# Attention ahead of two expert layers: the first pass one slot further ahead, the rows of maxima behind the products with v

## The chip, the cores and the metric

The kernel runs on one core of a Trainium2 chip. TensorE (PE in the profile, its weight loads PEld) multiplies, VectorE (DVE), ScalarE (ACT) and GpSimd (POOL) do the rest, and SyncE (SP) issues the DMAs. Each engine works through its own list of instructions in order; between engines there are semaphores. The metric is the device time of the whole program in microseconds, the median of several runs.

## The reference, cut to what matters

Queries are averaged in pairs, then attended over 1152 keys per head; what follows (two expert layers, called MoE below) is the same before and after the change.

```python
B, H, S, D = q.shape                              # 4, 8, 1152, 64
q_pool = q.reshape(B, H, S // 2, 2, D).mean(axis=3)      # 576 queries per head
scores = 1.0 / np.sqrt(D) * np.matmul(q_pool, k.transpose(0, 1, 3, 2))
scores = scores - np.max(scores, axis=-1, keepdims=True)
attn = np.exp(scores)
attn = attn / (np.sum(attn, axis=-1, keepdims=True) + 1e-09)
attn_out = np.matmul(attn, v)                     # then moe, then soft moe
```

## The kernel before

**Pairs, phases, slots.** The heads of a batch are taken two at a time: 16 pairs, each with two phases (one head each), each with nine slots (128 keys each). The loop over `s` runs through all slots; `u` is the slot's place in its pair, 0 to 17, `c` its place in its phase. The order of PE, ACT, DVE and POOL is the order of the program text (a manual schedule); the DMA queue on SP is ordered by the framework.

**Two passes.** The softmax needs each query's maximum before the exponentials. The first pass (`emit_S`, L189 and L190) multiplies 128 queries with 384 keys and lets DVE reduce the product to maxima, 27 such steps per pair; its products rotate through two buffers (`ps_s`). They are taken from one long list: `first()` emits the next. There is one `first()` in every slot and a second in every even slot, so the first pass runs ahead of the second by as many steps as were emitted before the loop. When all maxima of a group are there, `emit_nm` (L193, DVE) makes their negatives, and `emit_row` (L202 PE, L206 or L208 ACT) turns them with a matmul into a row that is copied into the tile `q2`. The second pass (`emit_E`, L218) multiplies keys with `q1` and with `q2` (which subtracts the maximum), and ACT takes the exponential (L221). `x0 = 1, n = 4` is the group of one head; `x0 = 0, n = 1` is a remainder of both heads of the next pair.

**Behind it.** POOL adds up the exponentials (`acc`, L225 and L227). In even slots PE multiplies the exponentials of two earlier slots with v (`emit_PV`, L234, eight matmuls); `emit_sum` (L244), `emit_recip` (L250, DVE) and `emit_O` (L259, L260, DVE) make the quotient of the phase before.

**The next pairs' operands.** `pool_q` (L105, two POOL additions) sums neighbouring queries into the tile `qp` at the end of slot u = 17, for the pair after next. `kq8` (L133, L109) transposes the last key block and the last query block at u = 1; its result is read by ACT (L140, L158, L159) and DVE (L141, L161). `q_bank` (L109, L118, L120) transposes the other query blocks, `k0` and `k4` (L133, L140, L141) the other key blocks, `kd_dma` (L168, L169) and `q2_dma` (L175) spread them by DMA. Transposes, rows and sums all take their output from `bank()`, which in the loop is the single buffer of the pool `ps_t`: the next user waits until the last reader of the one before is done.

```python
ps_s = ctx.enter_context(tc.tile_pool(name="ps_s", bufs=2, space=PSUM))
ps_t = ctx.enter_context(tc.tile_pool(name="ps_t", bufs=1, space=PSUM))
...
st["qp"] = kq_p.tile([128, 9, 2, 64], F32, tag="qp", name="qp")
```

Of the kernel before, what the change touches and what calls it, by code (L numbers as in the profile page):

```python
# [23 lines left out]
def attention(ctx, nc, tc, q, k, v, xa, ident, ones, hooks):  # L24
# [18 lines left out]
    NPH = 2 * NPAIR  # L43
# [36 lines left out]
    def load_v(pi):  # L80
        b, hp = pairs[pi]
        t = v_p.tile([128, 2, 9, 64], F32, tag="vr", name="vr")
        nc.sync.dma_start(
            out=t.rearrange("p h c d -> p h (c d)"),
            in_=v[b, 2 * hp:2 * hp + 2].rearrange("h (p c) d -> p h (c d)", c=9),
        )
        raws["v"][pi] = t
# [4 lines left out]
    def bank():  # L92
        if front[0]:
            return ps_e.tile([128, 512], F32, tag="se", name="t")
        return ps_t.tile([128, 512], F32, tag="t", name="t")
# [3 lines left out]
    def pool_q(pi, u):  # L99
        st = prep.setdefault(pi, {})  # L100
        if u == 0:
            st["qp"] = kq_p.tile([128, 9, 2, 64], F32, tag="qp", name="qp")
        qr = raws["q"][pi]
        eng = nc.gpsimd if pi else nc.vector
        eng.tensor_tensor(out=st["qp"][:, :, u, :], in0=qr[:, :, 0, :], in1=qr[:, :, 1, :], op=ALU.add)  # L105
# [7 lines left out]
    def q_bank(pi, g):  # L113
        st, ps = prep[pi], bank()
        q_tr(pi, 4 * g, 4, ps, 0)
        src = ps.rearrange("p (j h x) -> p h j x", j=4, h=2)
        o = st["q1"][:, :, g, :256].rearrange("p h (j x) -> p h j x", x=64)
        nc.scalar.copy(o, src)  # L118
        for h in range(2):
            nc.vector.tensor_tensor(  # L120
                out=o[64:128, h], in0=src[64:128, h], in1=o[64:128, h].bitcast(F32), op=ALU.subtract
            )
# [22 lines left out]
    def k0(pi):  # L145
        k_bank(pi, 0, 4, bank())

    def k4(pi):
        k_bank(pi, 4, 4, bank())

    def kq8(pi):
        ps = bank()
        k_bank(pi, 8, 1, ps)
        o, st = qd[pi % 2], prep[pi]
        src = ps[:, 128:256].rearrange("p (h g x) -> p h g x", h=2, g=2)
        q1 = st["q1"][:, :, :, 256:]
        for h in range(2):
            nc.scalar.copy(o[64 * h:64 * h + 64, 64 * h:64 * h + 64], ps[64 * h:64 * h + 64, 128 + 64 * h:192 + 64 * h])  # L158
        nc.scalar.copy(q1, src)  # L159
        for h in range(2):  # L160
            nc.vector.tensor_tensor(  # L161
                out=q1[64:128, h], in0=src[64:128, h], in1=q1[64:128, h].bitcast(F32), op=ALU.subtract
            )

    def kd_dma(pi, h):
        st, t = prep[pi], KD[(2 * pi + h) % 3]
        src = st["kp"][64 * h:64 * h + 64].bitcast(F32)
        nc.sync.dma_start(out=t[64:128, 0].bitcast(F32), in_=src[:, 0])  # L168
        ins = nc.sync.dma_start(out=t[0:64].bitcast(F32), in_=src)  # L169
        last_dma[0] = ins.ins  # L170
        return ins.ins

    def q2_dma(pi):
        st = prep[pi]
        return nc.sync.dma_start(out=st["q2"][0:64].bitcast(F32), in_=st["q1"][0:64].bitcast(F32)).ins  # L175


    def emit_S(ph, x, n):
        pi, h = divmod(ph, 2)
        st = prep[pi]  # L180
        if ph not in M_:
            M_[ph] = sm_p.tile([128, 5, 3], F32, tag="m3", name="m3")
        if x == 0:
            w, r = qd[pi % 2], st["kp"][:, 0]
        else:
            g, u = divmod(x - 1, 2)
            w, r = st["q1"][:, h, g, 128 * u:128 * u + 128], KD[ph % 3][:, 0]
        ps = ps_s.tile([128, 512], F32, tag="S", name="S")[:, :384]
        nc.tensor.matmul(ps, lhsT=w, rhs=r[:, 384 * n:384 * n + 384], start=True, stop=True)  # L189
        nc.vector.tensor_reduce(out=M_[ph][:, x, n:n + 1], in_=ps, axis=AX.X, op=ALU.max)  # L190

    def emit_nm(ph, x0, n):
        nc.vector.tensor_reduce(  # L193
            out=NM[ph % 2][:, x0:x0 + n, 64], in_=M_[ph][:, x0:x0 + n], axis=AX.X, op=ALU.max, negate=True
        )

    def emit_row(ph, x0, n):
        pi, h = divmod(ph, 2)
        q2 = prep[pi]["q2"][64:128]
        ps = bank()  # L200
        for x in range(n):
            nc.tensor.matmul(  # L202
                ps[:, 128 * x:128 * x + 128], lhsT=NM[ph % 2][:, x0 + x], rhs=identr, start=True, stop=True
            )
        if x0 == 0:
            nc.scalar.copy(q2[:, :, :, 256:], ps[64:128, :128].rearrange("p (h g x) -> p h g x", h=2, g=2))  # L206
        else:
            nc.scalar.copy(q2[:, h, :, :256], ps[64:128].rearrange("p (g x) -> p g x", g=2))  # L208


    def emit_E(ph, c):
        pi, h = divmod(ph, 2)
        st, kd = prep[pi], KD[ph % 3]
        e = E_[ph, c] = e_p.tile([128, 2, 288], F32, tag="e", name="e")
        for g in range(2):
            ps = ps_e.tile([128, 512], F32, tag="se", name="se")[:, :288]
            for z, y in enumerate((st["q1"], st["q2"])):
                nc.tensor.matmul(  # L218
                    ps, lhsT=kd[:, z, 128 * c:128 * c + 128], rhs=y[:, h, g], start=z == 0, stop=z == 1
                )  # L220
            nc.scalar.activation(out=e[:, g], in_=ps, func=AF.Exp, scale=1.0 / 16)  # L221

        if c == 1:
            acc_[ph] = sm_p.tile([128, 2, 288], F32, tag="acc", name="acc")
            nc.gpsimd.tensor_tensor(out=acc_[ph], in0=E_[ph, 0], in1=e, op=ALU.add)  # L225
        elif c > 1:
            nc.gpsimd.tensor_tensor(out=acc_[ph], in0=acc_[ph], in1=e, op=ALU.add)  # L227

    def emit_PV(ph, c):
        pi, h = divmod(ph, 2)  # L230
        if c == 0:
            O_[ph] = ps_o.tile([128, 512], F32, tag="o", name="o")
        for g in range(2):
            nc.tensor.matmul(  # L234
                O_[ph][64 * g:64 * g + 64, :288], lhsT=raws["v"][pi][:, h, c, :], rhs=E_[ph, c][:, g],
                start=c == 0, stop=c == 8,
            )
        E_.pop((ph, c))
# [9 lines left out]
    def emit_recip(ph, u):  # L248
        r = R_[ph][:, 144 * u:144 * u + 144]
        nc.vector.reciprocal(out=r, in_=r)  # L250
# [31 lines left out]
    def first(n=1):  # L282
        for _ in range(n):
            if firsts:
                emit_S(*firsts.pop(0))
# [4 lines left out]
    emit_row(0, 0, 1)  # L290
    emit_row(0, 1, 4)
    front[0] = False
    first()
    pool_q(1, 0)
    pool_q(1, 1)

# [2 lines left out]
    for s in range(SLOTS * NPH + 9):  # L299
        ph, c = divmod(s, SLOTS)  # L300
        pi, h = divmod(ph, 2)
        u = s % (2 * SLOTS)
        nxt, nn = pi + 1, pi + 2
        on = ph < NPH
        for f in hooks.get(s - SLOTS * NPH, ()):
            with tc.issue_after(last_dma[0]):
                f()
        if on:
            emit_E(ph, c)
        first()  # L310
        if ph + 1 < NPH:
            if u in (8, 17):
                emit_row(ph + 1, 1, 4)
            if u == 10:
                emit_row(ph + 1, 0, 1)
        if on and nxt < NPAIR:
            if s in (1, 2):
                (k0, k4)[s - 1](1)
            if u == (3 if s < 9 else 1):
                kq8(nxt)  # L320
                kd_dma(nxt, 0)
            elif u == 6:
                q_bank(nxt, 0)
            elif u == 11:
                q_bank(nxt, 1)
                q2_dma(nxt)
            elif u == 9:
                kd_dma(nxt, 1)
                load_v(nxt)
        if on and nn < NPAIR:  # L330
            if u == 13:
                k0(nn)
            elif u == 15:
                k4(nn)
        if s % 2 == 0:
            for g in (s - 3, s - 2):
                if 0 <= g < SLOTS * NPH:
                    emit_PV(*divmod(g, SLOTS))
            if ph and c in (3, 4):
                emit_sum(ph - 1)  # L340
            first()
        if ph and c in (5, 6):
            emit_recip(ph - 1, c - 5)
        if u == 8 and ph + 2 < NPH:
            emit_nm(ph + 2, 0, 1)
        if u in (6, 16) and ph + 1 < NPH:
            emit_nm(ph + 1, 1, 4)
        if ph and c == 7:
            emit_O(ph - 1)
        if on and nn < NPAIR:  # L350
            if u == 6:
                load_k(nn)
                load_q(nn)
            if u == 17:
                pool_q(nn, 0)
                pool_q(nn, 1)
# [761 lines left out]
```

## Time and profile before

| | |
|---|---|
| time, median of 3 runs | 2273.21 us (2272.35 to 2276.16) |
| the profiled execution | 2275.54 us, its span 2273.7 us, about 1.8 us around the span |
| PE busy | 2191.6 us, 96% of the span |
| PE weight loads (PEld) busy | 1970.6 us, 87% |
| DVE, ACT, POOL busy | 1436.3 (63%), 841.7 (37%), 583.8 (26%) |
| mean granted TensorE clock | 0.984 |

Attention takes the first quarter of the span. A row of the time line gives start and length in us, engine, line, operation and tiles, how many were merged (x4), and in brackets how long the engine had been idle and what it waited for. Matmuls are pipelined: the distance from one start to the next is what one costs, and the printed length contains the way out. Busy time of an engine that another one waits for counts only where that wait is the last to end.

### The profile page before, as it was taken

Reading aid. Unit: us, or ns where it says so; the run is one execution under the profiler, and the core shown is the slowest. Engines: PE = TensorE matmul, PEld = TensorE weight load, DVE = VectorE, ACT = ScalarE, POOL = GpSimd, SP = SyncE. Lnnn points to the kernel's source line nnn. Section 1 sums busy time; section 2 is a strip of 40 time slices with the busy share of each in tenths; the row PEclk is TensorE's granted clock in tenths of the full one; section 3 lists DMA queues with packets and bytes.
Section 4 is the critical chain, followed back from the end, with each engine's and each line's share of the span. In section 5 each row is a group of like instructions: output and inputs, shape, how many; then the busy total and the mean of one; then the engine's idle time right before and its main releaser. Section 6 shows DMA issues by size and latency. Waiting matters only on the chain.

```text
span 2273.7 us, 40984 instructions
## 1 busy us (share of the span) xinstructions
PE 2191.6 (96%) x16789; PEld 1970.6 (87%) x16789; DVE 1436.3 (63%) x2660; ACT 841.7 (37%) x1779; POOL 583.8 (26%) x368
## 2 busy tenths in 40 slices
PE   7999999999899999999999999999999999999986
PEld 5666666666899999999999999999999999988863
DVE  5777777775667766685586568558656855622321
ACT  3555555555433432342243234224233422312211
POOL 5777777777100300030030003003001300100000
PEclk9999999999999999999999999999999999999997
DMA  7544544542211211122131122212112221411169
GB/s 178 129 105 108 136 115 99 135 107 72 84 48 75 102 57 66 58 92 71 42 103 56 66 69 82 75 38 103 57 66 80 71 75 38 154 51 56 63 229 310
DMA packets 121194, 211.39 MB, mean 93 GB/s; under 512 B 43696, under 2 KB 95408, under 8 KB 109744
## 3 DMA queue, kind: packets, MB, share of 16 engines
q1 hardware_dynamic: 121008, 208.77, 30.3%
q8 instruction: 133, 2.18, 0.4%
q14 instruction: 53, 0.43, 0.1%
HBM read 161.56 MB, written 14.16 MB: 77 GB/s over the span
## 4 chain that ended last, share of the span: by engine, by line
PE 74%; DVE 13%; issue 9%; ACT 1%; DMA 1%; POOL 1%; SPq 0%; ACTq 0%; DVEq 0%; POOLq 0%
PE g L548 10%; PE g L549 10%; PE g L550 10%; PE y L577 7%; PE y L576 7%; PE y L575 7%; PE o L234 6%; PE se L218 5%; PE S L189 4%; DVE rs L250 3%; DVE m L190 2%; DVE ho L537 2%; DVE ht L530 2%; PE y L647 2%; PE y L649 1%
## 5 line engine op out<-in xcount | busy, mean ns | idle before, releaser
L548 PE MATMUL g<-xs,w 128*128 128x256 f32 x2304 | 660.2, 287 | 0.0
L550 PE MATMUL g<-xs,w 128*128 128x256 f32 x2304 | 654.3, 284 | 1.1 <-DVE w L443 1.1
L549 PE MATMUL g<-xs,w 128*128 128x256 f32 x2304 | 654.5, 284 | 0.0
L575 PE MATMUL y<-v,ho 128*128 128x256 f32 x1764 | 503.6, 285 | 9.1 <-ACT ho L536 9.1
L577 PE MATMUL y<-v,ho 128*128 128x256 f32 x1764 | 503.6, 285 | 6.8 <-DVE ho L537 6.8
L576 PE MATMUL y<-v,ho 128*128 128x256 f32 x1764 | 502.4, 285 | 0.0
L548 PEld LDWEIGHTS g<-xs,w 128*128 128x128 f32 x2304 | 445.2, 193 | 7.7 <-issue 7.0
L550 PEld LDWEIGHTS g<-xs,w 128*128 128x128 f32 x2304 | 444.7, 193 | 1.3 <-DVE w L443 1.3
L549 PEld LDWEIGHTS g<-xs,w 128*128 128x128 f32 x2304 | 445.1, 193 | 0.3
L564 ACT ACTIVATE hr<-g 128x512 f32<-128x512 f32 x252 | 150.5, 597 | 773.8 <-PE g L550 757.7
L443 POOL TENSOR_TENSOR w<-stg,w 128x1024 fp32r<-128x1024 f32 x28 | 68.1, 2433 | 1194.6 <-ACT w L442 1194.6
L530 DVE TENSOR_TENSOR ht<-hr 128x512 f32<-128x512 f32 x315 | 230.1, 764 | 223.8 <-ACT hr L564 221.4
L575 PEld LDWEIGHTS y<-v,ho 128*128 128x128 f32 x1764 | 341.5, 194 | 10.4 <-ACT ho L536 10.4
L577 PEld LDWEIGHTS y<-v,ho 128*128 128x128 f32 x1764 | 342.0, 194 | 8.3 <-DVE ho L537 8.3
L576 PEld LDWEIGHTS y<-v,ho 128*128 128x128 f32 x1764 | 341.7, 194 | 0.0
L227 POOL TENSOR_TENSOR acc<-acc,e 128x576 f32<-128x576 f32 x224 | 318.7, 1423 | 73.8 <-ACT e L221 64.5
L585 DVE SCALAR_TENSOR_TENSOR acc<-y,P,acc 128x256 f32<-128x256 f32 x540 | 244.2, 477 | 118.0 <-PE y L577 118.0
L190 DVE TENSOR_REDUCE m<-S 128x1 f32<-128x384 f32 x432 | 234.0, 549 | 115.2 <-PE S L189 103.5
L221 ACT ACTIVATE e<-se 128x288 f32<-128x288 f32 x576 | 207.2, 411 | 153.6 <-PE se L218 134.5
L537 DVE TENSOR_TENSOR ho<-ht,ho 128x512 fp32r<-128x512 f32 x315 | 258.5, 820 | 7.0 <-ACT ho L536 6.9
L218 PE MATMUL se<-q,kd 128*128 128x288 f32 x1152 | 219.5, 309 | 7.6 <-ACT q L208 7.3
L536 ACT CAST ho<-ht 128x512 fp32r<-128x512 f32 x315 | 188.8, 618 | 81.0 <-DVE ht L530 78.6
(177 smaller groups left out, 2364.0 us busy)
## 6 DMA issues: line engine op xcount, KB each, us to landing
xs<-xd SPq DMA_DIRECT2D x63, 1024.0 KB, 4.8
stg<-in_moe_w_dram SPq DMA_DIRECT2D x60, 512.0 KB, 5.8
kd<-kp SPq DMA_DIRECT2D x32, 576.0 KB, 5.8
m2w<-in_moe_w_dram SPq DMA_DIRECT2D x13, 1024.0 KB, 9.4
m2w<-in_moe_w_dram SPq DMA_DIRECT2D x22, 512.0 KB, 8.6
kr<-in_k_dram SPq DMA_DIRECT2D x32, 288.0 KB, 6.8
qr<-in_q_dram SPq DMA_DIRECT2D x16, 576.0 KB, 4.0
kd<-kp SPq DMA_DIRECT2D x32, 288.0 KB, 3.6
```

Source lines behind the costliest of these rows:

```text
L190: nc.vector.tensor_reduce(out=M_[ph][:, x, n:n + 1], in_=ps, axis=AX.X, op=ALU.max)
L218: nc.tensor.matmul(ps, lhsT=kd[:, z, 128 * c:128 * c + 128], rhs=y[:, h, g], start=z == 0, stop=z == 1)
L227: nc.gpsimd.tensor_tensor(out=acc_[ph], in0=acc_[ph], in1=e, op=ALU.add)
L530: nc.vector.tensor_tensor(out=src, in0=q[0], in1=q[1], op=op)
L537: nc.vector.tensor_tensor(out=o[:, 1], in0=src, in1=o[:, 0].bitcast(F32), op=ALU.subtract)
L548: nc.tensor.matmul(o, lhsT=w[:, 0, kk, c], rhs=x[:, 0, kk], start=kk == 0, stop=False)
L549: nc.tensor.matmul(o, lhsT=w[:, 0, kk, c], rhs=x[:, 1, kk], start=False, stop=False)
L550: nc.tensor.matmul(o, lhsT=w[:, 1, kk, c], rhs=x[:, 0, kk], start=False, stop=kk == 3)
L575: nc.tensor.matmul(ps, lhsT=o[:, 0, c], rhs=v[:, 0, c], start=c == 0, stop=False)
L576: nc.tensor.matmul(ps, lhsT=o[:, 0, c], rhs=v[:, 1, c], start=False, stop=False)
L577: nc.tensor.matmul(ps, lhsT=o[:, 1, c], rhs=v[:, 0, c], start=False, stop=c == 3)
L585: nc.vector.scalar_tensor_tensor(out=y, in0=ps, scalar=p, in1=y, op0=ALU.mult, op1=ALU.add)
```

## The change

Three steps of the first pass are emitted ahead of the loop after the first rows instead of one, so that the first pass is two steps, about one slot, further ahead. The negatives of a group are made one slot earlier. The row's matmuls move from slots 8, 17 and 10 (ahead of the products with v) to slots 6, 16 and 8, behind the products with v and the second step of the first pass. In slots 5 and 15 the negatives stand ahead of the reciprocal. The query transposes `q_bank(nxt, 0)` move from u = 6 to u = 2 (in the first phase of all to u = 5), `q_bank(nxt, 1)` and `q2_dma` from u = 11 to u = 10. `kq8` stays at u = 1 and `pool_q` at u = 17.

```diff
     front[0] = False
-    first()
+    first(3)
...
         first()
-        if ph + 1 < NPH:
-            if u in (8, 17):
-                emit_row(ph + 1, 1, 4)
-            if u == 10:
-                emit_row(ph + 1, 0, 1)
         if on and nxt < NPAIR:
             if s in (1, 2):
                 (k0, k4)[s - 1](1)
             if u == (3 if s < 9 else 1):
                 kq8(nxt)
                 kd_dma(nxt, 0)
-            elif u == 6:
+            elif u == (5 if s < 9 else 2):
                 q_bank(nxt, 0)
-            elif u == 11:
+            elif u == 10:
                 q_bank(nxt, 1)
                 q2_dma(nxt)
...
             if ph and c in (3, 4):
                 emit_sum(ph - 1)
             first()
+            if ph + 1 < NPH and u in (6, 16):
+                emit_row(ph + 1, 1, 4)
+            if ph + 2 < NPH and u == 8:
+                emit_row(ph + 2, 0, 1)
+        if u == 7 and ph + 2 < NPH:
+            emit_nm(ph + 2, 0, 1)
+        if u in (5, 15) and ph + 1 < NPH:
+            emit_nm(ph + 1, 1, 4)
         if ph and c in (5, 6):
             emit_recip(ph - 1, c - 5)
-        if u == 8 and ph + 2 < NPH:
-            emit_nm(ph + 2, 0, 1)
-        if u in (6, 16) and ph + 1 < NPH:
-            emit_nm(ph + 1, 1, 4)
```

## Rows read from the trace of the kernel before

**Rows 1.** Busy time of the engines in one stretch of attention: the stretch, its length, then PE, PEld, DVE, ACT, POOL busy (and instructions), granted clock, DMA share, GB/s.

```profile
200.00:300.00 100.00, 95.92 (x630) 67.70 (x631) 73.13 (x155) 55.25 (x150) 77.62 (x56) 1.00 0.53 120
```

**Rows 2.** Whom PE's matmuls waited for from 58 to 540 us: engine, line, releaser, then us in total, times, longest.

```profile
PE t L202 <- DVE nm L193: 11.5, 30, 0.8
PE se L218 <- ACT q L208: 7.3, 15, 0.5
PE S L189 <- DVE m L190: 1.5, 4, 0.6
```

**Rows 3.** PE's time line at the change from one pair to the next: the second pass of u = 17 starts at 256.57, the row at 258.12, u = 0 at 258.59, the products with v of u = 0 at 260.19, u = 1 at 261.59, the query transpose of `kq8` at 262.40, u = 2 at 262.43.

```profile
256.57 0.69 PE L218 MATMUL se<-q,kd 128*128 128x288 f32 x4
257.37 0.44 PE L189 MATMUL S<-kd,q 128*128 128x384 f32 x1
258.12 0.63 PE L202 MATMUL t<-identr,nm 128*128 128x128 f32 x4 [0.31 <-DVE nm L193]
258.59 0.34 PE L218 MATMUL se<-q,kd 128*128 128x288 f32 x1
259.42 0.66 PE L218 MATMUL se<-q,kd 128*128 128x288 f32 x3 [0.49 <-ACT q L208]
259.92 0.33 PE L189 MATMUL S<-kd,q 128*128 128x384 f32 x1
260.19 1.19 PE L234 MATMUL o<-e,vr 128*64 128x288 f32 x8
261.31 0.44 PE L189 MATMUL S<-kd,q 128*128 128x384 f32 x1
261.59 0.69 PE L218 MATMUL se<-q,kd 128*128 128x288 f32 x4
262.11 0.34 PE L189 MATMUL S<-kd,q 128*128 128x384 f32 x1
...
262.40 0.27 PE L109 MATMUL t<-ident,qp 128*128 128x128 f32 x1
262.43 0.77 PE L218 MATMUL se<-q,kd 128*128 128x288 f32 x4
263.04 0.34 PE L189 MATMUL S<-kd,q 128*128 128x384 f32 x1
```

**Rows 4.** ACT's time line there: a copy and the exponentials behind it, the exponentials of u = 17 (257.09), the row's copy (258.79).

```profile
254.57 0.59 ACT L140 CAST kp<-t 128x512 fp32r<-128x512 f32 x1
255.05 0.72 ACT L221 ACTIVATE e<-se 128x288 f32<-128x288 f32 x2
257.09 0.71 ACT L221 ACTIVATE e<-se 128x288 f32<-128x288 f32 x2 [1.32 <-PE se L218]
258.79 0.58 ACT L208 CAST q<-t 64x512 fp32r<-64x512 f32 x1 [0.99 <-PE t L202]
```

**Rows 5.** POOL's time line there: the last sum of the phase, then `pool_q`.

```profile
257.94 1.41 POOL L227 TENSOR_TENSOR acc<-acc,e 128x576 f32<-128x576 f32 x1 [0.43 <-ACT e L221]
259.31 2.79 POOL L105 TENSOR_TENSOR qp<-qr 128x576 f32<-128x576 f32 x2
```

**Rows 6.** DVE's time line there: the last reader of `k4`'s bank, the reciprocal behind it, and the last reader of `kq8`'s bank.

```profile
255.27 0.68 DVE L141 TENSOR_TENSOR kp<-t,kp 128x512 fp32r<-128x512 f32 x1
255.86 1.04 DVE L250 RECIPROCAL rs<-rs 128x144 f32<-128x144 f32 x1
...
264.14 0.37 DVE L161 TENSOR_TENSOR q<-t,q 64x64 fp32r<-64x64 f32 x2 [0.77 <-ACT q L159]
```

**Rows 7.** PE's time line at the other row of a pair (u = 8): first in the first pair, where the row doesn't wait, then in a later one.

```profile
42.39 0.34 PE L189 MATMUL S<-kp,qd 128*128 128x384 f32 x1
42.56 0.56 PE L202 MATMUL t<-identr,nm 128*128 128x128 f32 x4
43.05 1.19 PE L234 MATMUL o<-e,vr 128*64 128x288 f32 x8
...
273.05 0.34 PE L189 MATMUL S<-kp,qd 128*128 128x384 f32 x1
273.82 0.63 PE L202 MATMUL t<-identr,nm 128*128 128x128 f32 x4 [0.44 <-DVE nm L193]
```

**Rows 8.** The first pair, where two users of the single bank stand in neighbouring slots: the second one's start.

```profile
33.00 0.33 PE L133 MATMUL t<-ident,kr 128*128 128x128 f32 x1 [0.25 <-DVE kp L141]
```

**Rows 9.** The two stretches of attention at the lower granted clock (columns as in rows 1).

```profile
94.00:97.40 3.40, 3.40 (x13) 1.69 (x12) 0.56 (x1) 0.82 (x2) 2.37 (x2) 0.51 0.08 12
326.10:329.50 3.40, 3.40 (x15) 2.20 (x12) 0.92 (x2) 0.67 (x3) 1.60 (x2) 0.50 0.23 46
```

**Rows 10.** The chain that ended last, at the same place (products with v of u = 16) of several pairs: start, length, what.

```profile
86.17 1.12 PE o L234 x8
...
120.53 1.12 PE o L234 x8
...
153.33 1.12 PE o L234 x8
...
317.50 1.12 PE o L234 x8
...
351.89 1.12 PE o L234 x8
```

## The prediction, made before the change was run

> **What bounds the kernel now.** I read the busy time by stretch first. In a steady 100 us of attention PE is busy for 95.92, POOL for 77.62, DVE for 73.13, ACT for 55.25 [rows 1]: PE sets the pace, and what can be won is what PE waits. The list of waits names nearly all of it: the row of maxima waits for its negatives (11.5 us in 30 waits), the second pass waits for the row's copy (7.3 us in 15), a little is the first pass waiting for its buffers [rows 2]. Next the time line at the change of pair, where both happen. From the second pass of u = 17 (256.57) to the query transpose of `kq8` in u = 1 (262.40) 5.83 us go by [rows 3]. The reader is to see three holes there: the step of the first pass comes 0.80 behind the second pass where 0.52 is usual (261.59 to 262.11), the row 0.75 behind that, and the rest of the second pass 0.83 behind its first matmul. The pace of a pair, from the chain, is 153.33 - 120.53 = 32.80 us [rows 10]. Twice a pair took 34.36 and 34.39 us; there the granted clock was at 0.51 and 0.50, the lower of the two levels, for 3.4 us, right behind such a change of pair [rows 9]. So a fall of the clock costs 1.56 to 1.59 us.
>
> **What the change removes.** First the distances that PE keeps without a wait: first pass to what follows 0.17 (42.39 to 42.56) [rows 7]; second pass to first pass 0.52, or 0.61 behind a transpose; first pass to products with v 0.27; these to the next first pass 1.12; that to the second pass 0.28; first pass to the query transpose 0.29 [rows 3]. With the row gone from u = 17 and its copy done early, PE alone would go from the second pass of u = 17 to the transpose of `kq8` in 0.52 + 0.17 + 0.61 + 0.27 + 1.12 + 0.28 + 0.52 + 0.29 = 3.78 us instead of 5.83. The row itself isn't gone: its four matmuls, 0.47 (258.12 to 258.59), now stand at the end of u = 16. There they don't wait: the negatives are made right behind the last reader of `k4`'s bank, which ends at 255.95 and frees that bank too [rows 6], and in their new place the row would start at about 256.5, behind the step that precedes 256.57. At u = 8 the row came 0.77 behind the first pass where 0.17 is usual [rows 7]; that 0.60 goes as well, since the negatives of u = 5 no longer stand behind two reciprocals of 1.04 each. The reductions that the first pass needs for its two buffers are 0.5 us each and still finish within the same slots; I take no new wait from them (bound: 0 to 0.3 a pair, what is left of the 1.5 us in rows 2 on one side, the 0.28 above on the other).
>
> **What comes in the place of it: `qp`.** `kq8` at u = 1 needs `pool_q`, which stands behind the phase's last sum on POOL, which needs the exponentials of u = 17. This chain doesn't get shorter; it is the one thing at this place that is not moved. Counted from the second pass of u = 17: the row's copy on ACT now stands ahead of these exponentials. Copy behind row is 0.67 (258.12 to 258.79), second pass behind row 0.47, so the copy starts 0.20 behind the second pass [rows 3, 4]; it keeps ACT for 0.48 (a copy of the same length, 254.57 to 255.05), the two exponentials take 0.71, the sum starts 0.14 later (257.80 to 257.94) [rows 4, 5], `pool_q` 1.37 after that, and it lasts 2.79 [rows 5]; a hand-over to PE is 0.05 (copy's end 259.37 to 259.42) [rows 3, 4]. Together 0.20 + 0.48 + 0.71 + 0.14 + 1.37 + 2.79 + 0.05 = 5.74 us. Before, `qp` was ready at 262.10, just 0.30 before it was used [rows 3, 5], so there was almost no cover. After the change PE arrives at 3.78 and waits until 5.74: 1.96 us at the transpose, and behind it in PE's queue stands everything else. Of the way from 5.83 only 0.09 is won.
>
> The Trainium skill (GPSIMD Engine Reference, Performance versus the Vector engine) puts a two-input addition at about 2.6 cycles an element at 1.2 GHz; as an estimate from that page 576 elements take 1.25 us, three of them 0.4 us less than the rows have. The wait would then be 1.5 us and the total some 6 us lower. The rows show 1.37 to 1.41 us for one [rows 5]; they decide.
>
> **And the bank.** `q_bank(nxt, 0)` now follows `kq8` in the very next slot, with the same single bank. The last reader of `kq8`'s bank is DVE's L161, which ends at 264.14 + 0.37 = 264.51, 2.11 us behind the transpose at 262.40 [rows 3, 6]; this is a chain of ACT and DVE steps that wait for each other. PE is there 0.03 + 0.61 + 0.17 = 0.81 us behind the transpose [rows 3, 7]. With the hand-over it waits 2.11 + 0.05 - 0.81 = 1.35 us. That such a wait binds is seen in the first pair, where `k4` one slot behind `k0` waited for DVE's last read [rows 8]. At u = 6 the bank had long been free; that cover is gone. The products with v and all else of u = 2 are queued behind it. Bounds: 0, if the chain were done early, to 1.35; nothing in the rows lets it be shorter, so I take 1.35. The other moves (`q_bank(nxt, 1)` and `q2_dma` one slot earlier, the remainder's row at u = 8) meet a free bank and add no instruction: nothing. The key block for u = 8 is wanted a slot earlier, but the two new waits lie between its DMA and its use and give back more than that slot; nothing.
>
> **The sum.** Per change of pair: 5.74 for 5.83, the row 0.47 now ahead of it, 1.35 for the bank, less 0.60 at u = 8: -0.09 + 0.47 + 1.35 - 0.60 = +1.13 us. There are 14 with a `kq8`: +15.8. The fifteenth has none, and gains 5.83 - 3.78 - 0.47 = 1.6; the last pair's other row gains 0.6. The two extra steps ahead of the loop are taken from its end; their cost at the front I bound at -0.5 to +1 (a step and its reduction) and take as 0. Without the clock: +13.6.
>
> **The clock.** It fell in 2 of 15 changes of pair, each after holes of 0.28, 0.58 and about 0.7 us, some 1.6 in all. Now 1.96 and 1.35 us lie within 4.2 us, twice as much. So I expect a fall at most of them: 12 of 14. One that lies wholly on dense work costs 1.57; one that overlaps the second wait costs less, since a waiting PE loses nothing. I take 1.2: +14.4, bounds 0 and 14 x 1.57 = 22. The two falls of before go: -3.15.
>
> Total: 2275.54 + 13.6 - 3.15 + 14.4 = 2300.4 us for an execution like the profiled one. That one is 2.3 us above the median of the runs shown, so 2298.
>
> **Rivals.**
>
> 1. The waits come, but the clock falls nowhere in attention: 2273.2 + 13.6 - 3.15 = 2284. For it: the clock stayed up at 13 changes of pair. Against it: twice as much waiting at one place. The Trainium skill (TensorE: Matmul & The Clock Gate, Why this matters for your kernels) warns of long single gaps of the engine, and by its table holes as short as these would leave the clock up, which is this rival. The rows of before speak against it: the clock fell behind three holes that were each shorter still [rows 3, 9].
> 2. The bank is free in time, only `qp` binds: 14 x 1.35 = 18.9 less, 2279; with about half the falls 2272. For it: the chain to L161 has waits of its own. Against it: it was 2.11 us from the transpose with ACT and DVE both idle in between [rows 6].
> 3. Only the bank binds, `qp` is early enough (from the point where `pool_q` ends within 3.78 us): 3.78 for 5.83, so per pair -2.05 + 0.47 + 1.35 - 0.60 = -0.83, -11.6 in all; with five falls about 2264.
> 4. Neither binds and the change does what it says, on the other side: every pair loses its holes, -2.05 + 0.47 - 0.60 = -2.18 us, 14 x 2.18 + 2.2 + 3.15: 2273.2 - 35.9 = 2237. It decides if both `qp` within 3.78 us and the bank within 0.81 us are there. Against it: both chains were measured at 5.74 and 2.11.
>
> **How the numbers follow.** Chances: forecast 0.64, rival 1 0.10, rival 2 0.12, rival 3 0.04, rival 4 0.07, others 0.03. 0.2% is 4.5 us, about what a measurement of this kernel can tell from no change: 2268.7 to 2277.7 counts as the same. Faster: rivals 3 and 4, part of 2: 0.13. Same: part of 2 and others: 0.07. Slower: 0.80. The forecast's own range is 2284 to 2306; to leave out no more than rivals 3, 4 and the others it reaches to rival 2: 2272 to 2308.
>
> **What would show it.** The waits for L193 and L208 gone from PE's list; in their place L109 waiting for POOL's L105, 14 times about 2 us, and again L109 waiting for DVE's L161, 14 times about 1.3 us. A pair of 33.9 us, or about 35.3 where the clock falls; falls of the clock at most changes of pair. The prediction is wrong if L109 shows no wait for POOL, or if a pair takes less than 32.8 us.

## The result, and the profile after

| | before | after |
|---|---|---|
| time, median of 4 runs each | 2273.69 us (2272.35 to 2276.16) | 2301.08 us (2297.68 to 2301.45) |
| ratio | | 1.0114, 95% interval 1.0099 to 1.0129: slower |
| the profiled execution, its span | 2275.54, 2273.7 us | 2297.68, 2295.9 us |
| PE, PEld busy | 2191.6, 1970.6 us | 2192.9, 1969.8 us |
| DVE, ACT, POOL busy | 1436.3, 841.7, 583.8 us | 1433.0, 844.4, 582.4 us |
| mean granted TensorE clock | 0.984 | 0.984 |

No engine does more work. The waits of PE's matmuls from 58 to 570 us, in us in total, times, longest; they answer to [rows 2]:

```profile
PE t L109 <- POOL qp L105: 21.9, 14, 1.6
PE t L109 <- DVE q L161: 16.9, 14, 1.2
PE S L189 <- DVE m L190: 1.3, 3, 0.6
```

L202 and the wait for L208 are gone, as the change means. In their place the query transposes L109 wait twice at each of 14 changes of pair. In the busy time by stretch (columns as in [rows 1]) PE loses four to five points (95.92 to 91.35):

```profile
200.00:300.00 100.00, 91.35 (x599) 64.09 (x599) 68.15 (x146) 53.05 (x144) 73.89 (x53) 1.00 0.52 116
```

The time line at a change of pair answers to [rows 3 to 6]: all engines together, with weight loads and other rows left out.

```profile
266.69 0.56 PE L202 MATMUL t<-identr,nm 128*128 128x128 f32 x4
...
267.08 0.74 PE L218 MATMUL se<-q,kd 128*128 128x288 f32 x4
267.28 0.58 ACT L208 CAST q<-t 64x512 fp32r<-64x512 f32 x1 [1.40 <-PE t L202]
267.67 0.34 PE L189 MATMUL S<-kd,q 128*128 128x384 f32 x1
267.85 1.03 PE L218 MATMUL se<-q,kd 128*128 128x288 f32 x4
...
267.89 1.44 ACT L221 ACTIVATE e<-se 128x288 f32<-128x288 f32 x4
...
268.72 0.34 PE L189 MATMUL S<-kd,q 128*128 128x384 f32 x1
...
268.75 1.41 POOL L227 TENSOR_TENSOR acc<-acc,e 128x576 f32<-128x576 f32 x1 [1.11 <-ACT e L221]
...
270.11 2.77 POOL L105 TENSOR_TENSOR qp<-qr 128x576 f32<-128x576 f32 x2
...
271.10 0.27 PE L133 MATMUL t<-ident,kr 128*128 128x128 f32 x1
...
272.94 0.33 PE L109 MATMUL t<-ident,qp 128*128 128x128 f32 x1 [1.57 <-POOL qp L105]
273.03 0.77 PE L218 MATMUL se<-q,kd 128*128 128x288 f32 x4
...
273.64 0.33 PE L189 MATMUL S<-kd,q 128*128 128x384 f32 x1
...
274.66 0.37 DVE L161 TENSOR_TENSOR q<-t,q 64x64 fp32r<-64x64 f32 x2 [0.77 <-ACT q L159]
...
275.18 0.63 PE L109 MATMUL t<-ident,qp 128*128 128x128 f32 x4 [1.21 <-DVE q L161]
```

The row (266.69) starts 0.28 behind the first pass and doesn't wait; the second pass of u = 17 follows at 267.08. Its exponentials stand behind the row's copy on ACT and start at 267.89; the phase's last sum starts at 268.75, `pool_q` at 270.11, and ends at 272.88. PE is at the key transpose at 271.10 and can take the query transpose at 272.94 only: a hole of 1.84 us, where 0.11 is usual. Then `q_bank` in u = 2 finds the bank held until L161 ends at 275.03: 275.18 - 273.64 = 1.54, where 0.17 is usual. (A printed wait is shorter than the hole, since the matmul ahead of it is still on its way out.)

The chain at the same place of a pair gives its pace, as in [rows 10] (the place there and here is u = 14, not u = 16: these products stand behind the transposes of u = 13 and ahead of those of u = 15; the pace is the same). The first two points are a pair at the full clock, the other two one with a fall of the clock:

```profile
262.01 1.12 PE o L234 x8
...
296.43 1.12 PE o L234 x8
...
122.79 1.12 PE o L234 x8
...
158.71 1.12 PE o L234 x8
```

34.42 us a pair, where it had been 32.80, and 35.92 with a fall. The stretches at the lower granted clock in attention are three, where before there were two [rows 9]:

```profile
136.60:140.00 3.40, 3.40 (x14) 2.07 (x15) 1.33 (x3) 0.78 (x2) 0.96 (x1) 0.51 1.06 248
379.00:382.40 3.40, 3.40 (x14) 2.05 (x14) 1.33 (x3) 0.61 (x2) 1.05 (x1) 0.50 1.08 262
518.90:522.30 3.40, 3.11 (x12) 1.49 (x12) 1.47 (x4) 0.94 (x3) 1.40 (x1) 0.50 0.99 199
```

Where all of it went: the last sum of attention, PE's last wait for POOL there, starts at 576.86 where it had been 555.03 (PE's time lines, before first).

```profile
555.03 0.71 PE L244 MATMUL t<-acc,ones 128*64 128x288 f32 x4 [1.14 <-POOL acc L227]
```

```profile
576.86 0.71 PE L244 MATMUL t<-acc,ones 128*64 128x288 f32 x4 [1.16 <-POOL acc L227]
```

That is 21.8 of the 22.2 us between the spans; what comes behind takes 1719.0 us, before 1718.7. Of the 21.8, 14 x 1.62 = 22.7 are the slower pairs, about 1.5 the one additional fall, and -2.4 is what is left over: the place u = 14 of the first pair is 0.5 later than before (53.37 to 53.85), the last pair gains 1.8 (from 517.88 to the last sum it took 37.15, now 35.31 from 541.55), and -1.0 is not placed by these rows.

### The profile page after: what moved, and what is told of

It reads as the page before. It is cut to its first block, busy times and chain, and to the rows that moved or that the text cites. A ratio compares the mean times of both kernels' runs of the same rounds, so it can differ in the third digit from the quotient of the medians.

```text
span 2295.9 us, 40986 instructions
## 1 busy us (share of the span) xinstructions
PE 2192.9 (96%) x16789; PEld 1969.8 (86%) x16789; DVE 1433.0 (62%) x2660; ACT 844.4 (37%) x1779; POOL 582.4 (25%) x368
## 3 DMA queue, kind: packets, MB, share of 16 engines
q8 instruction: 133, 2.18, 0.4%
## 4 chain that ended last, share of the span: by engine, by line
PE 76%; issue 9%; DVE 8%; POOL 3%; ACT 2%; DMA 1%; SPq 0%; POOLq 0%; DVEq 0%; ACTq 0%
PE g L547 10%; PE g L548 9%; PE g L549 9%; PE y L576 7%; PE y L574 7%; PE y L575 7%; PE o L234 6%; PE se L218 6%; PE S L189 4%; DVE ho L536 2%; DVE ht L529 2%; POOL qp L105 2%; PE y L646 2%; PE y L648 1%; DVE v L467 1%
## 5 line engine op out<-in xcount | busy, mean ns | idle before, releaser
L218 PE MATMUL se<-q,kd 128*128 128x288 f32 x1152 | 223.8, 311 | 2.1 <-ACT e L221 0.3
```

Of the source, the lines that this page charges most:

```text
L218: nc.tensor.matmul(ps, lhsT=kd[:, z, 128 * c:128 * c + 128], rhs=y[:, h, g], start=z == 0, stop=z == 1)
```

## The experiments

The theory: the two waits of L109 are the whole loss, one for `qp`, one for the bank, and each can be taken away by itself. First rival: the row's copy, which now stands ahead of exponentials on ACT, holds PE back, and L109 only marks where. Second rival: the clock.

**1. `pool_q` earlier.** The tile `qp` is free once `q_bank(nxt, 1)` at u = 10 has read it.

```diff
-            if u == 17:
+            if u == 11:
                 pool_q(nn, 0)
                 pool_q(nn, 1)
```

> The changed kernel with one edit: the two additions of pool_q stand at the end of u = 11 instead of u = 17. Theory (two waits of the query transposes make the loss, the first for qp): in the changed kernel the transpose of kq8 starts 1.84 us behind the key transpose ahead of it, 0.11 would do; 14 x 1.73 = 24 us go, to about 2277, and PE's list of waits has no L109 behind POOL any more, while L109 behind DVE's L161 stays at 14 x 1.2 us. Rival (the row's copy on ACT, now ahead of the exponentials, is what holds PE, and L109 only shows where PE happens to stand): the wait moves to the second pass waiting for ACT, the time stays above 2293. Second rival (the clock): the time follows the number of falls, not this wait.

Measured: 2267.91 us (ratio to before 0.9973, 0.9963 to 0.9982), 33 us less than the changed kernel. Of PE's two waits the one for `qp` is gone; the other stays. Behind it two points of the chain, a pair apart:

```profile
PE t L109 <- DVE q L161: 18.0, 14, 1.3
...
86.80 1.12 PE o L234 x8
...
119.51 1.12 PE o L234 x8
```

A pair takes 32.71 us: 34.42 - 32.71 = 1.71, expected 1.73. The total moved by more. One part is the clock: in the profiled execution no fall is left in attention, where the changed kernel had three, about 4.5 us. With 14 x 1.71 = 23.9 that accounts for the 28.1 us between the two profiled spans; the medians are further apart because the other executions of the changed kernel are longer than its profiled one (below).

**2. The bank one slot later.**

```diff
-            elif u == (5 if s < 9 else 2):
+            elif u == (5 if s < 9 else 3):
                 q_bank(nxt, 0)
```

> The changed kernel with one edit: q_bank(nxt, 0) stands at u = 3 instead of u = 2 (all but the first phase), so that the single bank has one more slot to come free; pool_q stays at u = 17. Theory: the 1.54 us from the first pass to these transposes becomes 0.17 to 0.35, 14 x 1.2 to 1.37 = 17 to 19 us go, to about 2283; L109 behind POOL stays at 14 x 1.57 us. Rival (row's copy): no gain, above 2295. It could also be that u = 3 is still too early: then half of the gain, 2291.

Measured: 2271.73 us (0.9987, 0.9978 to 0.9997), 29 us less. Now only the other wait is there, as it was, and in the time line `q_bank` follows the first pass at once (266.12 to 266.30):

```profile
PE t L109 <- POOL qp L105: 22.0, 14, 1.6
```

```profile
261.38 0.27 PE L133 MATMUL t<-ident,kr 128*128 128x128 f32 x1
263.23 0.33 PE L109 MATMUL t<-ident,qp 128*128 128x128 f32 x1 [1.57 <-POOL qp L105]
...
266.12 0.34 PE L189 MATMUL S<-kd,q 128*128 128x384 f32 x1
266.30 0.60 PE L109 MATMUL t<-ident,qp 128*128 128x128 f32 x4
```

```profile
186.42 1.12 PE o L234 x8
...
219.35 1.12 PE o L234 x8
```

A pair takes 32.93, 1.49 less, somewhat more than the 1.2 to 1.37 expected, again with no fall in the attention of the profiled execution.

**3. Both.**

> The changed kernel with both edits: pool_q at u = 11 and q_bank(nxt, 0) at u = 3. Theory: both waits go, 24 + 18 = 42 us, to about 2259, below the kernel before (2274), at 31.4 us a pair; the waits for the negatives and the row's copy stay gone. What could be late next is the first pass waiting for its buffers behind DVE: up to 0.3 a pair, 2263. Rival (row's copy): above 2290.

Measured: 2247.05 us (0.9883, 0.9868 to 0.9897), 54 us less than the changed kernel and 27 less than the one before. The two waits are gone together and nothing of their size took their place:

```profile
200.00:300.00 100.00, 99.61 (x661) 71.09 (x659) 75.97 (x164) 58.08 (x157) 80.08 (x58) 1.00 0.56 128
```

```profile
209.73 1.12 PE o L234 x8
...
240.88 1.12 PE o L234 x8
```

A pair takes 31.15 to 31.17 us (expected 31.4). The first rival falls as the main cause: the row's copy is still where the change put it. So does the second: these are pairs at the full clock, as was the one of 34.42 us. The two savings add up: 1.71 + 1.49 = 3.20, together 3.25. Against the kernel before, 1.63 us a pair are won by what the change was about.

**4. The bank's wait by itself**, in the kernel before.

```diff
-            elif u == 6:
+            elif u == (6 if s < 9 else 2):
                 q_bank(nxt, 0)
```

> The kernel before with one part of the change alone: q_bank(nxt, 0) at u = 2 instead of u = 6 (all but the first pair); rows, negatives and first pass as before. Theory: the bank's wait comes by itself, L109 behind L161 about 14 x 1.2 us, 14 x 1.37 = 19 us slower, about 2293. Rival (the wait exists only because PE arrives late from the wait for qp, or because of the row's copy): no such wait, 2274.

Measured: 2290.48 us (1.0074, 1.0059 to 1.0089). The wait is there without any of the rest, beside those of before:

```profile
PE t L109 <- DVE q L161: 17.9, 14, 1.3
PE t L202 <- DVE nm L193: 7.9, 30, 0.4
PE se L218 <- ACT q L208: 7.3, 15, 0.5
```

A pair takes 34.02, 1.22 more, not 1.37: the waits for L193 came down from 11.5 [rows 2] to 7.9 us, so part of the new hole was given back there.

**5. `pool_q` earlier in the kernel before** (at the end of u = 12, since there `q_bank(nxt, 1)` stands at u = 11).

```diff
-            if u == 17:
+            if u == 12:
                 pool_q(nn, 0)
                 pool_q(nn, 1)
```

> The kernel before with one edit: pool_q at the end of u = 12 instead of u = 17 (its q_bank(nxt, 1) stands at u = 11). Theory: in the kernel before qp was ready 0.30 us before its use, so it set nothing; the pair stays at 32.80 us, 2274 within 4 us. Rival (qp on POOL was already part of what set the pace before): 10 us or more faster.

Measured: 2275.22 us beside 2275.56 of the kernel before on that chip (0.9999, 0.9990 to 1.0009); a pair takes 32.80 to 32.83. `qp` set nothing before; its 0.30 us of cover was enough there, and only there.

**6. The kernel of experiment 3 once more**, as the neighbour of the next one.

> The kernel of the run with both edits once more, as the neighbour of the next one on the same chip: a pair of 31.17 us, 2247.

Measured: 2245.47 us in one run, a pair of 31.15.

**7. What is left: the row's copy.** In experiment 3 the second pass of the next slot follows each row at once (259.64); that of the slot after it takes 0.89 us (260.39 to 261.28) where 0.65 is usual:

```profile
259.64 0.74 PE L218 MATMUL se<-q,kd 128*128 128x288 f32 x4
260.22 0.34 PE L189 MATMUL S<-kp,qd 128*128 128x384 f32 x1
260.39 1.05 PE L218 MATMUL se<-q,kd 128*128 128x288 f32 x4
261.28 0.34 PE L189 MATMUL S<-kd,q 128*128 128x384 f32 x1
```

The copy of the row of u = 6 is put behind the exponentials of u = 7:

```diff
         if on:
             emit_E(ph, c)
+            while late:
+                late.pop()()
...
-                emit_row(ph + 1, 1, 4)
+                emit_row(ph + 1, 1, 4, u == 6)
...
-        else:
+        elif later:     # the row of u == 6
+            late.append(lambda: nc.scalar.copy(q2[:, h, :, :256], ...))
+        else:
             nc.scalar.copy(q2[:, h, :, :256], ps[64:128].rearrange(...))
```

> The kernel with both edits and one more: the copy of the row of u = 6 stands on ACT behind the exponentials of u = 7 instead of ahead of them. Theory: behind each row the second pass two groups on takes 0.89 us where 0.65 is usual, because the copy holds back the exponentials that free its three buffers; one of two rows of a pair is mended, 15 x 0.24 = 3.6 us, a pair of 30.93, about 2243.5. Rival (the 0.24 is the row's own weight load or the first pass behind DVE): no gain.

Measured: 2243.90 us (0.9861, 0.9844 to 0.9877 of before), the fastest of all. At that place the distance is 0.65 again (258.96 to 259.61); behind the other row, whose copy stayed, it is 0.88 (276.20 to 277.08). L222 is the L218 of the other kernels:

```profile
258.96 0.81 PE L222 MATMUL se<-q,kd 128*128 128x288 f32 x4
259.61 0.34 PE L189 MATMUL S<-kd,q 128*128 128x384 f32 x1
...
276.20 1.04 PE L222 MATMUL se<-q,kd 128*128 128x288 f32 x4
277.08 0.34 PE L189 MATMUL S<-kd,q 128*128 128x384 f32 x1
```

A pair takes 30.93, 0.22 less (expected 0.24). The total against the single run of experiment 6 went down by only 1.6; the attention part, from the first pair to its last sum, by 3.4. So the copy's place costs 0.2 us at this row, and the first rival is right to that extent.

**8. One long hole.** In experiment 2's kernel the second addition of `pool_q` is done twice, so POOL is 1.4 us later.

```diff
                 pool_q(nn, 0)
                 pool_q(nn, 1)
+                pool_q(nn, 1)
```

> The changed kernel with q_bank(nxt, 0) at u = 3 and the second addition of pool_q done twice (1.4 us of POOL more, same result): one single hole per change of pair, 1.84 + 1.37 = 3.2 us instead of 1.84. By itself 14 x 1.37 = 19 us more than the run with q_bank at u = 3, about 2291, with no fall of the clock if single holes of this size leave it up. If what counts is the sum of the waiting at one place, as the prediction took it, 3.2 us should bring falls at most changes of pair: 10 to 14 falls, 15 to 21 us more, 2306 to 2312.

Measured: 2307.39 us in one run. From the key transpose to the query transpose it is now 3.30 us, and the clock falls at 12 of 14 changes of pair; without a fall the distance from one query transpose to the next is 34.4, with one 35.7 to 36.0. The mean granted clock in the same stretch as above, then two of the falls:

```profile
200.00:300.00 100.00, 90.50 (x568) 63.39 (x567) 65.59 (x143) 50.48 (x136) 73.73 (x54) 0.95 0.51 116
280.40:283.80 3.40, 3.40 (x16) 2.26 (x11) 1.59 (x5) 1.70 (x5) 1.40 (x1) 0.50 0.96 282
314.50:317.90 3.40, 2.99 (x12) 2.10 (x14) 1.22 (x4) 1.56 (x6) 2.12 (x3) 0.50 0.57 159
```

So falls at nearly every change, as the prediction had them, come with one hole of 3.3 us. They didn't come with the two of the changed kernel, which are 1.84 + 1.54 = 3.38 us together: three falls in 14 changes of the profiled execution.

## Why the prediction was right, and where its terms were not

The time, 2298 predicted and 2301 measured, was right, and so were the two waits and their places. That these waits cost more in every pair than the change wins there is the mechanism as forecast. That the total came so near is luck: in the profiled execution the pairs cost 6.9 us more than forecast and the clock some 9.9 less, so two wrong terms nearly cancelled.

- **`qp`.** The way from the second pass of u = 17 to the query transpose was put at 5.74 us; it is 5.86 (267.08 to 272.94). The links are as they were read [rows 4, 5], but the exponentials start 0.81 behind the second pass, not 0.68, since the copy keeps ACT for 0.61 (267.28 to 267.89), not 0.48. PE would have been there after 4.13 us (0.11 behind 271.10), not 3.78, mostly because of the 0.24 behind the row (below); so 5.86 - 4.13 = 1.73 us are waited, not 1.96. Experiment 1 gives 1.71 for it.
- **The bank.** Put at 1.35, the hole exceeds the usual by 1.37; experiment 2 gives 1.49, experiment 4 1.22 without the rest.
- **The row.** Predicted at 0.47 in its new place, 0.28 + 0.39 + 0.59 up to the next first pass less the usual 0.28 + 0.52 makes 0.46. But the prediction took no cost for its copy standing ahead of exponentials except on POOL's chain. Experiment 7 shows it: 0.22 us at the row of u = 6. At u = 16 the same delay of PE lies inside the wait for `qp` and costs nothing while that wait is there.
- **What went at u = 8** was taken from one pair as 0.60 [rows 7]; it is 0.60 to 0.63 in 12 of the 15 rows that wait there, so this term was right.
- **A pair** was thus 1.62 us slower, not 1.13: 22.7 us in all instead of 15.8. The mis-sized parts are 0.12 on the way to `qp`, 0.24 behind the row of u = 6, and some 0.08 at the bank (2.24 from one transpose to the other, put at 2.16). The remaining 0.05 is not placed.
- **The clock.** This term failed: 12 new falls at 1.2 us were predicted, 14.4 us less the 3.15 of the old ones: 11.25 us. There are three in the profiled execution, at 1.5 us each, one more than before: 1.35 us. The step that failed is "twice as much waiting at one place, so a fall at most changes". Single holes of 1.6 us (experiment 1) and 1.84 us (experiment 2) brought none in 14 changes each, both together 3 in 14, three holes of 0.28, 0.58 and about 0.7 us two in 15 [rows 9]; only the hole of 3.30 us of experiment 8 brought 12. The other three executions of the changed kernel are some 3.5 us longer than the profiled one, at a mean clock of 0.981 beside 0.984. By the time that would be two more falls, by the mean clock about four of 3.4 us; there is no trace of them, so how many falls they had in attention stays open.
- **The rivals.** Rival 1 (both waits, the clock as good as untouched) was nearest in its mechanism, though its 2284 is 17 us too low: 6.9 for the pairs, some 4.5 for the three falls that it leaves out, and the rest because it starts from the median before, while the profiled execution was 2.3 above it before and 3.4 below the median after. The page of the Trainium skill that it named (TensorE: Matmul & The Clock Gate, Why this matters for your kernels) comes out better for single holes than the prediction had it: those of 1.6 and 1.84 us left the clock up, the one of 3.3 didn't. Rival 4 is what the change would have been with `qp` and the bank taken along: -2.18 us a pair was computed for it; experiment 3 has -1.63, and most of the 0.55 between them is the row's copy, twice 0.24 (one shown by experiment 7, the other by the same distance behind the other row).
- **POOL's price.** The prediction's estimate from the Trainium skill (GPSIMD Engine Reference, Performance versus the Vector engine) put the wait at 1.5 us. The wait printed is 1.57 and 1.73 in the prediction's count, but that does not bear the estimate out: POOL's additions took 1.36 to 1.41 us each, as in the rows of before, where the estimate had 1.25. The wait is shorter than 1.96 because PE came later, not because POOL was quicker.

## What to carry to other kernels

When a wait on the bounding engine is removed, look at what that engine reaches next, and how much cover each operand had there: `qp` had 0.30 us, and a gain of two us per pair ran straight into it. A step that is moved takes its buffer along: in a pool of one buffer ask when the last reader of the neighbour in front is done (here 2.1 to 2.2 us through ACT and DVE), not when its matmuls are. Moving both, the producer ahead and the second user of the bank one slot back, turned 1.1% slower into 1.2% faster, and with one copy put behind the exponentials it was 1.4%.

## What the runs showed of the hardware that was not expected

That the granted clock stays at its upper level through one hole of 1.84 us every 33 us (none of 14 changes fell), yet fell in the kernel before behind three holes that were each shorter (2 of 15), and at 12 of 14 behind one hole of 3.30 us. Experiment 4 has both kinds, some 5 us apart: its three falls in attention (from 60.3, 469.9 and 507.4 on) all begin right behind the short holes of the row, none behind its 14 holes of 1.6 us. Why two holes of 1.84 and 1.54 us, 0.70 us of work apart, brought it down at 3 of 14 changes and not at the others isn't settled by these runs. A fall lasted 3.4 us and cost 1.3 to 1.6 us in attention, in all these kernels.
